# The sums of w_out's quarters: from GpSimd and VectorE to VectorE alone, every second pass, and later in the scheduler's order

## The chip, the cores and the metric

The kernel runs on one core of a Trainium2 chip. The metric is the device time of one execution in microseconds. Times below are the median of several runs where so called; everything that comes from the profile belongs to one profiled execution, which has its own time. Engine names are those of the profile: PE (matrix), DVE (VectorE), ACT (ScalarE), POOL (GpSimd), SP (the engine that issues the DMAs here).

## The reference, cut to what matters

Attention over 8 batches of 8 heads with 512 local tokens and 32 global ones (a local token sees a window of 32 to each side and the global tokens; a global one sees all), then a feed-forward layer over the 4608 tokens:

```python
    attn_out = _attn_ref(**attn_kwargs)                 # 8 x 8 x 544 x 64
    x = np.ascontiguousarray(attn_out.transpose(0, 2, 1, 3)).reshape(B * S, H * D)
    h = x @ w_in                                        # 512 -> 2048
    g = np.where(h > 0.0, h, alpha * (np.exp(np.minimum(h, 0.0)) - 1.0))
    return (g @ w_out).astype(np.float32)               # 2048 -> 512
```

The weights come as 64-bit floats. The kernel splits every value of `x`, of `g` and of the two weights into a high and a low float16 part, scaled by powers of two, and makes each product out of three float16 products.

## The kernel before, in words

**Attention** is a generator of slots (batch, pair of head pairs, tile of 128 tokens). Scores go to PSUM (L626, L574), DVE adds the mask and takes the maximum (L638), ACT makes the exponentials (L645), POOL divides by the sum (L652), PE transposes (L663), the transposed tile is copied to SBUF (L666), and PE multiplies with v (L685). The result is one 256-token block of `x` after the other.

**The feed-forward layer** is a second generator, `ffn_stream`. It works on jobs of one block, and a job on passes: pass `p` (0 to 7) takes the hidden columns of `p` (256 of them). `ffn1` issues 24 matmuls of 128x256 into `h` (L293), then ACT makes `g`, `hs` and the exponential (L302 to L304), DVE joins them (`elu`, L311), ACT makes the high part `gh`, DVE the low part `gl` (L314). Up to `LAG2` = 2 passes later `ffn2` multiplies with w_out, 12 matmuls of 128x512 into two banks `acc` (L368). At the end of a job DVE adds `acc` to the earlier partial result `o` (L376).

**Groups of weights.** w_in and w_out arrive and are converted in four groups of passes: a (0), b (1), c (2, 3), d (4 to 7). Early blocks run one group at a time, and their partial results go to DRAM and back. Once all weights are there, a later block runs all passes in one job, "f", and its second product goes by seven products of 128x256 quarters in place of eight (`ffn2_seven`, L408).

**The sums of quarters** are what these seven products need. `add_up(p, False)`, here called a pair, makes two sums for pass `p` ("rows" and "diag"); `add_up(p, True)`, a cross sum, replaces the middle of w_out's own rows by two differences, and may do so only when no job of the old kind will use pass `p` any more. One call has four steps, each deferred by two ticks against the one before:

- `s0` (L250): `w` = high part + low part of w_out, 128x1024, float16 to float32, on POOL
- `s1` (L254 for a cross sum; L256 and L257 for a pair): the sums or the difference out of `w`, on DVE, 128x512 and 128x256
- `s2` (L261): the high float16 part, on ACT
- `s3` (L265): the low float16 part, on DVE

The tile `w` is one of three buffers named `cu`, of which two hold the diag sums for good, so that only one `w` can be alive. The tiles of `s1` are three buffers named `tmp`. The results lie in `raw` (rows), `cu` (diag) and w_out itself (`wouth`, `woutl`).

**Who calls.** `load()` stands at the head of every pass. Once the table "f" exists it starts one pair if any is left, and one cross sum if its pair was started and pass `p` is free. There are 8 pairs and 8 cross sums.

**What sets the order.** The program is written as the two generators step (by the table `PACE`); small steps are put off by `defer`, and `tick` runs those that are due. The tile layer then orders the instructions of each engine by priority, which is by default the place in the program, and by what it reckons to be ready. `tc.high_priority(offset=n)` moves the instructions inside it n places ahead; a negative n moves them back. On the chip each engine runs its list strictly in order.

Of the kernel before, what the change touches and what calls it, by code (L numbers as in the profile page):

```python
# [29 lines left out]
NP = NFT // 2  # L30
# [7 lines left out]
CONV = 14  # L38
NBL = B * SL // BLK
GROUPS = {"a": (0, 1), "b": (1, 2), "c": (2, 4), "d": (4, 8), "f": (0, 8)}  # L40
NX = 4


# [10 lines left out]
def attn_ffn(ctx: ExitStack, tc: tile.TileContext, qT, qgT, kT, vT, w_in, w_out, mask, out):  # L54
    nc = tc.nc
# [22 lines left out]
    def defer(n, fn):  # L78
        if n == 0:
            return fn()  # L80
        later.setdefault(now[0] + n, []).append(fn)
# [38 lines left out]
    wout = [wz[:, 256:].rearrange("p (f e) -> p f e", f=NFT), wts.tile([P, NFT, DM], F16, name="woutl")]  # L120
# [9 lines left out]
    def load_weights(group):  # L130
        lo, hi = GROUPS[group]
        for p in range(lo, hi):
            for m in range(2):
                unit(m, p)
                if (m, p) == (1, hi - 1):
                    defer(12, lambda: tables(group))
                    if hi == NP:
                        defer(13, lambda: tables("f"))
                yield
# [62 lines left out]
    def tables(group):  # L202

        r = slice(*GROUPS[group])
        wm = wts.tile([P, 4], F32, name=f"wm_{group}")
# [28 lines left out]
    def add_up(p, cross):  # L234


        if not sums:
            sums["rows"] = [ffn.tile([P, NP * 512], F16, name="raw") for _ in range(2)]
            sums["diag"] = [ffn.tile([P, NP * 256], F16, name="cu", bufs=3) for _ in range(2)]
        w = ffn.tile([P, 2, DM], F32, name="cu", bufs=3)  # L240
        s = ffn.tile([P, 512], F32, name="tmp", bufs=3)
        d = None if cross else ffn.tile([P, 512], F32, name="tmp", bufs=3)[:, 0:256]
        pr = slice(2 * p, 2 * p + 2)
        flat = [a[:, pr, :].rearrange("p a b -> p (a b)")[:, 256:768] for a in wout]
        rows = [a[:, p * 512:(p + 1) * 512] for a in sums["rows"]]
        diag = [a[:, p * 256:(p + 1) * 256] for a in sums["diag"]]
        todo = ((flat, s),) if cross else ((rows, s), (diag, d))

        def s0():
            nc.gpsimd.tensor_add(w, wout[0][:, pr, :], wout[1][:, pr, :])  # L250

        def s1():
            if cross:
                nc.vector.tensor_sub(s, w[:, 1, :], w[:, 0, :])  # L254
            else:
                nc.vector.tensor_add(s.rearrange("p (a b) -> p a b", a=2), w[:, :, 0:256], w[:, :, 256:512])  # L256
                nc.vector.tensor_add(d, w[:, 0, 0:256], w[:, 1, 256:512])  # L257

        def s2():
            for dst, src in todo:  # L260
                nc.scalar.copy(dst[0], src)  # L261

        def s3():
            for dst, src in todo:
                nc.vector.tensor_sub(dst[1], src, dst[0])  # L265
            if cross:
                added.append(p)

        for i, fn in enumerate((s0, s1, s2, s3)):
            defer(1 + 2 * i, fn)  # L270

    added = []
    uses = [0] * NP
# [3 lines left out]
    def ffn_stream():  # L277
        pend = []
        state = {}
# [67 lines left out]
        def ffn2():  # L347
            job, p, gh, gl = pend.pop(0)
            group, blk, _, _, sc, seven = job
            first, last = GROUPS[group][0], GROUPS[group][1] - 1  # L350
            if seven is not None:
# [32 lines left out]
        def ffn2_seven(blk, p, gh, gl, sc, done):  # L384
            while p not in added:
                load()
                yield True
# [50 lines left out]
        def split_x(blk):  # L438
            xr, mx = ready[blk]
            xh = ffn.tile([P, NC, BLK], F16, name="xh", bufs=NX)  # L440
            xl = ffn.tile([P, NC, BLK], F16, name="xl", bufs=NX)
            done = []
            xf, hf, lf = (a.rearrange("p c t -> p (c t)") for a in (xr, xh, xl))

            def s1():
                all_max(mx[:, 1:2], mx[:, 0:1])

            def s2():
                nc.vector.tensor_scalar_max(mx[:, 1:2], mx[:, 1:2], LOW)
                power(mx[:, 2:3], mx[:, 1:2])  # L450
                nc.vector.reciprocal(mx[:, 3:4], mx[:, 2:3])
                nc.vector.tensor_scalar_mul(mx[:, 4:5], mx[:, 3:4], 2.0 ** 14)
                nc.scalar.activation(hf, xf, AF.Copy, scale=mx[:, 4:5])  # L453

            def s3():
                nc.vector.scalar_tensor_tensor(out=lf, in0=xf, scalar=mx[:, 4:5], in1=hf,
                                               op0=ALU.mult, op1=ALU.subtract)
                done.append(1)

            nc.vector.tensor_reduce(out=mx[:, 0:1], in_=mx[:, 6:10], op=ALU.max, axis=AX.X)  # L460
            lag = 6 if "f" in tab else 2
            for i, fn in enumerate((s1, s2, s3)):
                defer(lag + i, fn)
            return xh, xl, mx, done

        def scales(group, mx):
            sc = ffn.tile([P, 3 * NP + 1], F32, name="xs", bufs=4)
            wm, t = tab[group]
            o = GROUPS[group]
            r = slice(*o)  # L470
# [11 lines left out]
        def load():  # L482
            if "f" in tab:
                n = state.setdefault("sums", 0)
                if n < NP:
                    add_up(n, False)
                    state["sums"] += 1
                n = state.setdefault("cross", 0)
                first = min((GROUPS["abcd"[step[b]]][0] for b in order if 0 < step[b] < 4), default=NP)
                if n < state["sums"] and not uses[n] and n < first:  # L490
                    add_up(n, True)
                    state["cross"] += 1
            for blk in order:
                if blk in ready and blk not in xs and not step[blk] and len(xs) < NX:
                    xs[blk] = split_x(blk)

        def choose():

            for blk in order:
                if blk in xs and xs[blk][3] and step[blk] < 4:  # L500
                    group = "f" if "f" in tab and not step[blk] else "abcd"[step[blk]]
                    if group in tab:
# [3 lines left out]
                        if seven is None:  # L506
                            for p in range(*GROUPS[group]):
                                uses[p] += 1
# [4 lines left out]
        while lead[0]:  # L513
            load()
            yield True
        while left <= NBL:
            load()
            job = job or choose()
            if job is None:
                yield True  # L520
                continue
            cur, job = job, None
            group, blk = cur[:2]
            lo, hi = GROUPS[group]
            for p in range(lo, hi):
                load()
                yield from ffn1(cur, p)
                if len(pend) > LAG2:
                    yield from ffn2()
                if p == hi - 1:  # L530
                    job = choose()
            if group in "df":
                del xs[blk]
                left += 1
# [6 lines left out]
    def new_x():  # L541
        return ffn.tile([P, NC, BLK], F32, name="xr", bufs=3), ffn.tile([P, 10], F32, name="xm", bufs=NX + 4)

# [315 lines left out]
```

## Time and profile before

| what | value |
|---|---|
| median of 3 runs | 1045.69 us |
| lowest and highest | 1040.73 and 1049.07 us |
| the profiled execution's own time | 1048.61 us |
| its span, first to last instruction | 1046.8 us |
| mean granted PE clock | 0.963 |
| busy: PE, DVE, ACT, POOL | 977.8, 788.2, 687.1, 273.5 us |
| start of the first and the last L250 on POOL | 200.7 and 299.0 us |

The profile is read by stage. The sums lie between about 200 and 375 us of a program of 1047 us, so the shares over the whole span say little of them; what counts is which engine the others wait for in those stretches. "PEclk" is the share of full speed that PE's clock was granted. In the lists of instructions a row is start, duration, engine, line, operation, tiles, and in brackets the idle time ahead of it and what ended that. In the chain of waits a row is start, length and what ran. A duration there is the time until the next link starts, so it is the price of one instruction in a row of many.

### The profile page before, as it was taken

The numbers are of one execution on the slowest core, as the hardware profiler recorded it, in microseconds if no ns is written. First come the engines' busy times: TensorE is split into PE (matmuls) and PEld (weight loads), VectorE is DVE, ScalarE is ACT, GpSimd is POOL, SyncE is SP. The second block draws the span as 40 slices with busy tenths as digits, with TensorE's granted clock in tenths as the row PEclk, the third lists the DMA queues.
The fourth block names the chain that finished last, engine by engine and source line by source line (L and its number), as shares of the span: only waits on it lengthen the run. The fifth ranks groups of instructions, "written<-read, shape, count | busy, mean of one in ns | idle before, by whom it ended". The sixth has DMA issues, their size and how long they took to land.

```text
span 1046.8 us, 21647 instructions
## 1 busy us (share of the span) xinstructions
PE 977.8 (93%) x8128; PEld 781.1 (75%) x8128; DVE 788.2 (75%) x2217; ACT 687.1 (66%) x1561; POOL 273.5 (26%) x458
## 2 busy tenths in 40 slices
PE   6898869889689999999999999999999999999995
PEld 4576546556357678888888888888888888888884
DVE  5789899977865677878786778868787778676573
ACT  4779778655444666667676767667576766677663
POOL 2356574237451112121122112112122121100000
PEclk9799989979689999999999999999999999999998
DMA  7546665531122112311131022101220100000000
GB/s 264 166 127 206 222 224 184 183 112 56 40 76 66 47 41 77 102 27 41 67 102 31 16 90 83 47 22 37 84 89 22 42 21 32 1 22 22 1 22 21
DMA packets 39168, 81.95 MB, mean 78 GB/s; under 512 B 3864, under 2 KB 5912, under 8 KB 39064
## 3 DMA queue, kind: packets, MB, share of 16 engines
q1 hardware_dynamic: 39064, 80.58, 23.5%
q8 instruction: 64, 1.05, 0.4%
q14 instruction: 40, 0.33, 0.1%
HBM read 65.36 MB, written 15.20 MB: 77 GB/s over the span
## 4 chain that ended last, share of the span: by engine, by line
PE 59%; DVE 21%; ACT 11%; issue 3%; POOL 3%; DMA 1%; DVEq 0%; ACTq 0%; POOLq 0%
PE h L293 20%; PE acc L408 9%; PE h L408 5%; PE pa L663 4%; PE pa L626 4%; PE pa L685 4%; ACT p L645 3%; PE pa L293 3%; PE acc L368 3%; DVE p L638 3%; DVE gl L314 3%; DVE g L311 3%; PE pa L574 2%; PE pa L408 2%; ACT g L302 2%
## 5 line engine op out<-in xcount | busy, mean ns | idle before, releaser
L293 PE MATMUL h<-xh,winh 128*128 128x256 f16 x992 | 273.4, 276 | 10.5 <-ACT xh L453 5.9
L293 PE MATMUL h<-xl,winh 128*128 128x256 f16 x992 | 273.2, 275 | 0.1
L293 PE MATMUL h<-xh,winl 128*128 128x256 f16 x992 | 273.0, 275 | 0.0
L293 PEld LDWEIGHTS <-winh 128*128 128x128 f16 x2176 | 213.0, 99 | 51.9 <-issue 22.5
L652 POOL TENSOR_SCALAR p<-p,sm 128x224 f32<-128x224 f32 x256 | 141.8, 573 | 302.9 <-DVE sm L650 145.1
L311 DVE SCALAR_TENSOR_TENSOR g<-g,hs 128x512 f32<-128x512 f32 x136 | 99.8, 734 | 98.5 <-ACT g L304 97.7
L645 ACT ACTIVATE p<-p,m 128x224 f32<-128x224 f32 x256 | 120.2, 472 | 70.7 <-DVE m L641 69.3
L408 PEld LDWEIGHTS <-gh 128*128 128x128 f16 x1456 | 141.8, 98 | 21.0 <-issue 4.8
L302 ACT ACTIVATE g<-h,xs 128x512 f32<-128x512 f32 x124 | 85.0, 685 | 55.7 <-PE h L293 55.1
L293 PEld LDWEIGHTS <-winl 128*128 128x128 f16 x1088 | 107.4, 99 | 13.7 <-issue 0.4
L314 DVE SCALAR_TENSOR_TENSOR gl<-gs,xs,gh 128x640 f16<-128x640 f32 x104 | 94.2, 906 | 23.1 <-ACT gh L333 22.9
L333 ACT ACTIVATE gh<-gs,xs 128x640 f16<-128x640 f32 x104 | 86.4, 831 | 38.3 <-DVE gs L329 38.3
L332 ACT ACTIVATE gh<-g,xs 128x256 f16<-128x256 f32 x104 | 53.3, 513 | 77.2 <-DVE g L311 77.2
L304 ACT ACTIVATE g<-g 128x512 f32<-128x512 f32 x136 | 85.9, 632 | 0.0
L303 ACT ACTIVATE hs<-h,xs 128x512 f32<-128x512 f32 x124 | 84.8, 684 | 0.0
L663 PE MATMUL pa<-ident,p 128*128 128x128 f32 x512 | 79.6, 283 | 4.1 <-POOL p L652 4.0
L314 DVE SCALAR_TENSOR_TENSOR gl<-g,xs,gh 128x256 f16<-128x256 f32 (+1 forms) x136 | 77.7, 572 | 4.6 <-ACT gh L318 4.4
L408 PEld LDWEIGHTS <-gl 128*128 128x128 f16 x728 | 71.2, 98 | 13.0 <-DVE gl L314 0.5
L638 DVE CUSTOM_DVE_ANT_0 p<-pa,msk 128x224 f32<-128x224 f32 x228 | 76.5, 383 | 4.6 <-PE pa L626 4.5
L408 PE MATMUL acc<-raw,gh 128*128 128x256 f16 x416 | 79.4, 273 | 0.0
L666 DVE COPY pt<-pa 128x512 f32<-128x512 f32 x98 | 66.6, 680 | 13.8 <-PE pa L663 13.7
L626 PE MATMUL pa<-k,q 64*128 64x224 f32 x456 | 68.5, 400 | 3.2 <-ACT pt L666 2.2
(194 smaller groups left out, 2048.5 us busy)
## 6 DMA issues: line engine op xcount, KB each, us to landing
v<-vT SPq DMA_DIRECT2D x64, 256.0 KB, 2.7
k<-kT SPq DMA_DIRECT2D x32, 448.0 KB, 4.0
out<-o SPq DMA_DIRECT2D x34, 256.0 KB, 2.1
q<-qT SPq DMA_DIRECT2D x32, 256.0 KB, 5.0
raw<-w_in SPq DMA_DIRECT2D x8, 1024.0 KB, 6.0
raw<-w_out SPq DMA_DIRECT2D x8, 1024.0 KB, 5.3
od<-o SPq DMA_DIRECT2D x24, 256.0 KB, 2.5
o<-od SPq DMA_DIRECT2D x24, 256.0 KB, 3.3
```

Source lines behind the costliest of these rows:

```text
L293: nc.tensor.matmul(h[:, j, :], wt[:, c, f], xt[:, c, :], start=k == 0, stop=k == 11)
L302: nc.scalar.activation(g, hf, AF.Relu, scale=sc[:, p:p + 1])
L304: nc.scalar.activation(g, g, AF.Exp, scale=-1.0)
L311: nc.vector.scalar_tensor_tensor(out=g, in0=g, scalar=-1.0, in1=hs, op0=ALU.add, op1=ALU.max)
L314: nc.vector.scalar_tensor_tensor(out=dst, in0=src, scalar=sg, in1=hi, op0=ALU.mult, op1=ALU.subtract)
L333: nc.scalar.activation(gh[:, 2:7, :], s, AF.Copy, scale=sg)
L408: nc.tensor.matmul(cols, gt, w, start=first, stop=p == NP - 1 and k == len(todo) - 1)
L626: nc.tensor.matmul(sp[r][:, j * KW:(j + 1) * KW], q[rows, t * P:(t + 1) * P], k[rows, t, :], start=True, stop=True)
L638: nc.vector.tensor_tensor_reduce(out=p[:, 0:KW], in0=sp[r][:, j * KW:(j + 1) * KW], in1=msk[:, mi, :], op0=ALU.add, op1=ALU.max, scale=1.0 ...
L645: nc.scalar.activation(ps[i][:, 0:KW], ps[i][:, 0:KW], AF.Exp, bias=m[:, 1, i:i + 1], scale=scale, accum_out=s[:, 0, i:i + 1])
L652: nc.gpsimd.tensor_scalar(ps[i][:, 0:KW], ps[i][:, 0:KW], s[:, 1, i:i + 1], 1.0, ALU.mult, ALU.mult)
L663: nc.tensor.transpose(tp[:, (2 * r + i) * P:(2 * r + i + 1) * P], ps[2 * j + r][:, i * P:(i + 1) * P], ident)
```

## The change

Three things are changed: `s0` is issued on DVE in place of POOL; all four steps of a sum are issued under a priority of 60 places further back; and `load()` starts a pair at every second call only (a cross sum still at every call, once its conditions hold).

```diff
@@ -38,6 +38,7 @@
+BEHIND = 60
@@ -247,7 +248,7 @@
         def s0():
-            nc.gpsimd.tensor_add(w, wout[0][:, pr, :], wout[1][:, pr, :])
+            nc.vector.tensor_add(w, wout[0][:, pr, :], wout[1][:, pr, :])
@@ -266,8 +267,12 @@
+        def behind(fn):
+            with tc.high_priority(offset=-BEHIND):
+                fn()
+
         for i, fn in enumerate((s0, s1, s2, s3)):
-            defer(1 + 2 * i, fn)
+            defer(1 + 2 * i, lambda fn=fn: behind(fn))
@@ -482,7 +487,8 @@
         def load():
             if "f" in tab:
                 n = state.setdefault("sums", 0)
-                if n < NP:
+                state["turn"] = not state.get("turn")
+                if n < NP and state["turn"]:
                     add_up(n, False)
                     state["sums"] += 1
```

Line numbers after the change are higher by one to six: L250, L254, L265, L311, L314 and L376 become L251, L255, L266, L316, L319 and L381. DVE's list has 16 instructions more, POOL's 16 fewer, and PE's list is in the same order from about 240 us on. From the pass whose tile is `g_3744` on DVE's list is the same but for names.

The first of two places is DVE, one pass in the middle of the sums. The names carry buffer numbers: a `tmp` made from a `cu` is `s1`, a `raw`, `cu` or `woutl` made from a `tmp` is `s3`. Before:

```order
L311 SCALAR_TENSOR_TENSOR g_2876<-g_2876,hs_2877 128x512
L265 TENSOR_TENSOR raw_2771<-tmp_2842,raw_2770 128x512
L265 TENSOR_TENSOR cu_2773<-tmp_2843,cu_2772 128x256
L314 SCALAR_TENSOR_TENSOR gl_2882<-g_2876,xs_2700,gh_2881 128x512
L265 TENSOR_TENSOR woutl_109<-tmp_2845,wouth_107 128x512
L256 TENSOR_TENSOR tmp_2911<-cu_2910 128x512
L257 TENSOR_TENSOR tmp_2912<-cu_2910 128x256
L254 TENSOR_TENSOR tmp_2914<-cu_2913 128x512
L311 SCALAR_TENSOR_TENSOR g_2945<-g_2945,hs_2946 128x512
```

And now, the same pass:

```order
L316 SCALAR_TENSOR_TENSOR g_2866<-g_2866,hs_2867 128x512
L257 TENSOR_TENSOR tmp_2895<-cu_2894 128x512
L258 TENSOR_TENSOR tmp_2896<-cu_2894 128x256
L319 SCALAR_TENSOR_TENSOR gl_2872<-g_2866,xs_2700,gh_2871 128x512
L251 TENSOR_TENSOR cu_2897<-wouth_107,woutl_109 128x1024
L266 TENSOR_TENSOR raw_2771<-tmp_2895,raw_2770 128x512
L255 TENSOR_TENSOR tmp_2898<-cu_2897 128x512
L266 TENSOR_TENSOR cu_2773<-tmp_2896,cu_2772 128x256
L251 TENSOR_TENSOR cu_2962<-wouth_107,woutl_109 128x1024
L316 SCALAR_TENSOR_TENSOR g_2929<-g_2929,hs_2930 128x512
```

Both `w` of a pass (`cu_2897`, `cu_2962`) now stand in DVE's list, each between the steps that need it and those that free its buffer. `gl` is two rows behind `g` where it was three.

The second place is DVE again, some five passes on, at a block's low part `xl` (beside it stand steps of attention). Before, no step of a sum stands within this stretch; `s1` of three late cross sums stood a few rows ahead of it. Now:

```order
L257 TENSOR_TENSOR tmp_3626<-cu_3625 128x512
L647 TENSOR_SCALAR m_3320<-m_3320 128x4
L107 TENSOR_SCALAR xm_2504<-xm_2504 128x1
L258 TENSOR_TENSOR tmp_3627<-cu_3625 128x256
L456 RECIPROCAL xm_2504<-xm_2504 128x1
L251 TENSOR_TENSOR cu_3864<-wouth_107,woutl_109 128x1024
L457 TENSOR_SCALAR xm_2504<-xm_2504 128x1
L266 TENSOR_TENSOR raw_2771<-tmp_3626,raw_2770 128x512
L255 TENSOR_TENSOR tmp_3865<-cu_3864 128x512
L251 TENSOR_TENSOR cu_3970<-wouth_107,woutl_109 128x1024
L461 SCALAR_TENSOR_TENSOR xl_3251<-xr_2503,xm_2504,xh_3250 128x1024
```

The last pair (`cu_3625`) and two of the late cross sums have moved to the front of `xl`, which is on the way of the next block into the feed-forward layer. Over the nine passes from `g_2809` to `g_3484` DVE's list holds 13 times L251, `s1` of 7 pairs and 6 cross sums, and `s3` of 8 pairs and 4 cross sums.

## The prediction

> **What bounds the kernel now.** I read the page's slices first, to find the stretch in which PE isn't full, then the table by windows for that stretch, and then the instructions in it.
>
> ```profile
> span 1046.8 us, 21647 instructions
> PE   6898869889689999999999999999999999999995
> DVE  5789899977865677878786778868787778676573
> ```
>
> A slice is 26.2 us. From the thirteenth on (314 us) PE is at nine tenths or more in all but the last slice; up to there it is not. The sums of w_out lie in slices 8 to 12, and the eleventh (262 to 288 us) has PE at 6 beside DVE at 8.
>
> ```profile
> core 0: us, PE busy (x) PEld busy (x) DVE busy (x) ACT busy (x) POOL busy (x), PEclk, DMA share, GB/s
> 251.00:260.00 9.00, 9.00 (x66) 6.35 (x65) 6.70 (x10) 4.26 (x8) 4.97 (x3) 1.00 0.01 2
> 260.00:269.00 9.00, 5.70 (x18) 2.06 (x17) 8.65 (x10) 3.84 (x8) 4.55 (x3) 0.69 0.00 0
> 269.00:278.00 9.00, 3.10 (x23) 2.39 (x22) 9.00 (x12) 4.40 (x9) 5.08 (x3) 0.88 0.00 1
> ...
> 241.00:322.00 81.00, 65.48 (x411) 41.54 (x410) 61.23 (x106) 37.56 (x80) 40.09 (x33) 0.85 0.21 66
> 322.00:343.00 21.00, 21.00 (x159) 14.68 (x160) 10.48 (x26) 10.78 (x25) 2.87 (x7) 1.00 0.09 26
> ```
>
> From 260 to 278 us DVE is busy 17.65 of 18 us and PE gets through 41 matmuls, at a reduced clock. Between 322 and 343 us PE is full at full clock: 21.00 us for 159 matmuls, 0.132 us each. At that price the 411 matmuls from 241 to 322 us are 54.3 us of work, in a stretch of 81: **about 26 us are lost to PE there**. The chain of waits gives the same price from another side:
>
> ```profile
> 235.89 2.62 PE h L293 x24
> ...
> 348.31 2.59 PE acc L368 x12
> ```
>
> A pass of the feed-forward layer is 24 + 12 matmuls, 5.21 us. Nine of them are 46.9 us; what attention puts between them makes up the rest of 54.3. Who makes PE wait is told by the groups of this stretch:
>
> ```profile
> L368 PE MATMUL acc<-wouth,gl 128*128 128x512 f16 x35 | 15.8, 451 | 2.8 <-DVE gl L314 2.8
> L368 PE MATMUL acc<-wouth,gh 128*128 128x512 f16 x34 | 15.1, 443 | 9.0 <-DVE o L376 8.5 <-ACT gh L318 0.5
> ```
>
> It is DVE each time, with steps that cost it 0.7 us and come late. Late behind what, the list of DVE and POOL shows:
>
> ```profile
> 259.51 2.50 POOL L250 TENSOR_TENSOR cu<-wouth,woutl 128x1024 f32<-128x1024 f16 x1 [0.81 <-DVE tmp L254]
> 277.52 2.12 POOL L250 TENSOR_TENSOR cu<-wouth,woutl 128x1024 f32<-128x1024 f16 x1 [2.56 <-DVE tmp L257]
> ...
> 259.35 0.69 DVE L311 SCALAR_TENSOR_TENSOR g<-g,hs 128x512 f32<-128x512 f32 x1
> 259.95 2.61 DVE L265 TENSOR_TENSOR raw<-tmp,raw 128x512 f16<-128x512 f32 x1
> 275.43 0.68 DVE L265 TENSOR_TENSOR raw<-tmp,raw 128x512 f16<-128x512 f32 x1
> 277.96 2.22 DVE L311 SCALAR_TENSOR_TENSOR g<-g,hs 128x512 f32<-128x512 f32 x1
> ```
>
> The same instruction takes 0.68 us alone and 2.61 us when it starts inside an L250 of POOL; L311 takes 0.69 and 2.22. Each of the two long ones ends within 0.6 us of the end of POOL's. So while POOL adds, a DVE instruction with two operands in SBUF stands still. Where none of these falls into an L250, DVE waits for its result (the waits of this stretch, with us in total, times, longest; the two rows below it are used further down):
>
> ```profile
> DVE tmp L254 <- POOL cu L250: 9.3, 4, 2.7
> PE acc L368 <- DVE o L376: 8.5, 3, 6.0
> ...
> DVE raw L265 <- ACT raw L261: 0.4, 1, 0.4
> ```
>
> Either way **an addition on POOL costs DVE about 2 us**, two of them a pass, and a pass takes 9 us (L311 starts at 259.35 and, two passes later, at 277.96) where PE needs 5.2.
>
> The Trainium skill, "SBUF — State Buffer", on the two sides of SBUF, says that DVE and GpSimd share a pair of ports as an exclusive lock, held for a whole instruction, and that a DVE instruction with two SBUF inputs falls under it; the trace agrees, 2.22 against 0.69 us.
>
> **The change part by part.** *Taken from POOL.*
>
> ```profile
> L250 POOL TENSOR_TENSOR cu<-wouth,woutl x16: 2117/2124/2507, 200.7 to 299.0; 128x1024 f32<-128x1024 f16 x16
> ```
>
> Fourteen of the 16 start after 241 us. At 2 us each DVE gets back 28 us of standing still, close to the 26 us that PE loses. POOL has nothing else that is waited for in the FFN-only passes.
>
> *Added to DVE.* A 128x1024 addition of two float16 tiles into float32 isn't in the trace on DVE. The nearest rows, as prices in a row of work:
>
> ```profile
> 203.40 0.60 DVE cu L163
> 205.32 1.14 DVE cu L166
> 211.82 0.60 DVE tmp L256
> 277.04 0.34 DVE tmp L257
> 263.50 0.66 DVE gl L314
> 268.51 0.60 DVE g L311
> ```
>
> L166 has two tensors of 128x1024, 1.14 us; L163 has one, 0.60 us. From 256 to 512 columns (L257, L256) the price grows by 0.26 us, which carried on to 1024 gives 0.60 + 0.53 = 1.13. I take 1.14, since two tensors are read; 0.60 is the lower end.
>
> The Trainium skill, "VectorE: DVE Perf Modes", on what auto-detection checks, lets an instruction with two tensors run at double rate only if every tensor is 16-bit; the float32 result here would rule that out. By it the price stays at 1.14; with the double rate, 13 additions would give DVE 7 us back.
>
> *Moved on DVE.* I price its list over the nine passes from `g_2809` to `g_3484`, which before are the stretch from 241 to 322 us. Sums: 13 L251 at 1.14 = 14.8; `s1` of 7 pairs at 0.94 = 6.6 and of 6 cross sums at 0.60 = 3.6; `s3` of 8 pairs at 0.94 = 7.5 and of 4 cross sums at 0.60 = 2.4. Together 34.9 us. The rest of DVE's work there is as before:
>
> ```profile
> L314 DVE SCALAR_TENSOR_TENSOR gl<-g,xs,gh 128x512 f16<-128x512 f32 x10 | 8.9, 893 | 0.0
> L311 DVE SCALAR_TENSOR_TENSOR g<-g,hs 128x512 f32<-128x512 f32 x9 | 7.9, 877 | 0.0
> L376 DVE SCALAR_TENSOR_TENSOR o<-acc,xs,o 128x512 f32<-128x512 f32 x5 | 3.6, 739 | 0.0
> L666 DVE COPY pt<-pa 128x512 f32<-128x512 f32 x4 | 2.7, 681 | 1.8 <-PE pa L663 1.8
> L638 DVE CUSTOM_DVE_ANT_0 p<-pa,msk 128x224 f32<-128x224 f32 x8 | 2.7, 385 | 0.6 <-PE pa L626 0.6
> ```
>
> At undisturbed prices `gl` is 6.6 and `g` 5.4; with the three others 21.0 us, and I put the small ones (a block's `xl`, reductions, statistics) at 4. Sum: 34.9 + 25 = **60 us of DVE against 54 us of PE**. So DVE stays the bound of this stretch, by little, and PE should be short of work by some 6 us in place of 26. In a pass without attention such as `g_2866` to `g_2929`, DVE has 6.1 us against PE's 5.2; over the first five passes 27 against 26, which the two passes of lead of `ffn1` can hide; the passes before and at `xl_3251` have 7 to 9 us of DVE, beside attention's matmuls on PE.
>
> *The waits.* Both engines near full, each hand-off can cost. The added wait is none by itself: `w` is now freed and refilled within one engine, where POOL and DVE took turns. What is left is `s3`, which waits for ACT's cast. Before, that cost 0.4 us in all; behind it now stand `gl`, `o` and the next `w`, and PE waits for the first two. I put 3 us for such waits, half a hand-off a pass, between 0 and 12. So the stretch takes 60 + 3 = 63 us in place of 81: **-18**.
>
> *Before 241 us.* Two additions fall into the conversion of the last weights, and DVE is on the chain there with both instructions that they hold up:
>
> ```profile
> 201.22 2.18 DVE g L311
> 213.58 2.00 DVE gl L314
> ```
> ```profile
> 238.62 0.73 DVE L311 SCALAR_TENSOR_TENSOR g<-g,hs 128x512 f32<-128x512 f32 x1 [1.59 <-ACT g L304]
> ```
>
> Undisturbed these are 0.60 and 0.66, so 2.9 us come back; two additions of 1.14 go in, the first on the chain in place of 0.94 that moves behind it, the second ahead of the 1.59 us for which DVE idles before 238.62. **-2**, between 0 and -4.
>
> *Every second pass.* The pairs now spread over eight passes and not seven: the scheduler takes them ahead again where it sees DVE free. Priced in the list above, so nothing more. *The place 60 back*: `gl` two rows behind `g`, not three; in the list too.
>
> *After 322 us* PE is full (21.00 of 21.00), and its list is the same, so the time saved stays saved; late cross sums leave DVE 10.5 of 21 us busy there, and it can take the lag up.
>
> Sum, against the profiled execution's 1048.6 us: -18 - 2 = 1028.6, which is 1.9% less. The median shown lies 2.9 us below that execution; carried over, the prediction is **1026 us**.
>
> **The rivals.** *PE becomes the bound at once.* If the addition costs 0.60 us, DVE's 60 us fall to 53, and the stretch is PE's 54.3: -26 with -3 before it, 1017. For it speaks that PE is full right after; against it the two-tensor row of 1.14.
>
> *DVE keeps PE waiting.* DVE has more work than PE, and a stall of 2.8 us at 261 us was followed by a granted clock of 0.69. If `o` and `gl` still come late at each of the five `o`, waits are 12 us and not 3: -9 and 0, 1037. For it: `o` alone made PE wait 8.5 us. Against it: 6.0 of these were one wait in which POOL held DVE several times.
>
> *Slower: `s3` holds DVE.* DVE's list is strict. If each cast stands in ACT's list behind the three ACT instructions of a pass, DVE waits for these first:
>
> ```profile
> 383.20 0.69 ACT g L302
> 383.89 0.58 ACT hs L303
> 384.46 0.53 ACT g L304
> ```
>
> That is 1.8 us for each of the 20 `s3` (8 pairs of two, 4 cross): 36 us, 60 + 36 = 96 in place of 81, and with -2 that makes 1059. It decides from (81 - 60) / 20 = 1.05 us a cast. Against it: in the list, `gl`, another `s1` or a `w` stand between most `s1` and their `s3`, and ACT was busy only 37.56 of 81 us.
>
> *The gain is given back.* Were something later bound by transfers or by the pace of attention, the 20 us would turn into idle time there: 1046. Against it speaks the full PE after 322 us.
>
> **How the numbers follow.** A measurement of this kernel can tell about 1% from no change, which is 1035.2 us. Chances: the forecast (1020 to 1033) 0.60; PE the bound 0.13; PE kept waiting 0.17, about half of it under 1035; given back 0.06; slower 0.04. So faster by over 1% 0.81, within 1% 0.15, slower 0.04. The range is 1016 to 1038: from the faster addition to five late `o`; beyond it lie the last two cases.
>
> **What would show it.** POOL without L250 and no `g` or `gl` over 1 us in the whole trace; L251 on DVE at 1.1 to 1.2 us; from 241 us to `g_3484` 60 to 66 us, with DVE over 90% busy; the eleventh slice of PE at 8 or 9 and its clock near 10; the same PE rate after. Wrong would be: `s3` long idle for ACT, PE waiting over 10 us for `o` and `gl` together, or the saved time coming up as idle PE after 330 us.

## The result, and the profile after

| | before | after |
|---|---|---|
| median | 1045.28 us (4 runs) | 1017.18 us (4 runs, 1015.35 to 1018.12) |
| ratio, with its 95% interval | | 0.9731 (0.9689 to 0.9772) |
| the profiled execution's own time | 1048.61 us | 1018.12 us |
| busy: PE, DVE, ACT, POOL | 977.8, 788.2, 687.1, 273.5 us | 965.1, 785.8, 685.9, 247.0 us |
| mean granted PE clock | 0.963 | 0.977 |

The kernel is 28 us faster, where 20 were forecast: the time lies within the range (1016 to 1038), at its fast end, and outside the 1020 to 1033 that had been called the likeliest. The page of the kernel after, span and slices:

```profile
span 1016.3 us, 21648 instructions
...
PE   6898879989999999999999999999999999999994
...
DVE  5789898999986778677777778787787878766663
...
PEclk9799999989999999999999999999999999999998
```

The hole in PE's row (the 6 and the 8 from 262 us on) is gone, and DVE is at 9 in the slices of the sums up to the eleventh. The windows of the nine passes, which now run from 234.9 to 294.6 us, and of the stretch behind them:

```profile
core 0: us, PE busy (x) PEld busy (x) DVE busy (x) ACT busy (x) POOL busy (x), PEclk, DMA share, GB/s
...
235.00:295.00 60.00, 58.45 (x423) 39.84 (x422) 59.83 (x121) 37.96 (x83) 15.86 (x19) 1.00 0.26 85
295.00:312.00 17.00, 17.00 (x132) 11.93 (x130) 10.19 (x27) 9.49 (x22) 4.49 (x7) 1.00 0.09 28
```

DVE has 59.83 of 60 us busy, and still PE is full but for 1.55 us, at full clock. The same instructions on DVE as shown before, and what PE and DVE waited for:

```profile
L251 DVE TENSOR_TENSOR cu<-wouth,woutl x16: 1191/1212/1239, 209.8 to 295.7; 128x1024 f32<-128x1024 f16 x16
```

```profile
257.18 0.68 DVE L316 SCALAR_TENSOR_TENSOR g<-g,hs 128x512 f32<-128x512 f32 x1
...
259.70 0.68 DVE L266 TENSOR_TENSOR raw<-tmp,raw 128x512 f16<-128x512 f32 x1
```

```profile
PE pa L112 <- DVE xm L465: 1.0, 1, 1.0
DVE gl L319 <- ACT gh L323: 1.0, 1, 1.0
...
PE acc L373 <- DVE o L381: 0.4, 1, 0.4
```

The addition takes 1.21 us on DVE where it took 2.12 on POOL; in the nine passes no `g`, `gl` or step of a sum is longer than the shortest of its kind by more than 0.26 us; `s3` (L266) waits for ACT not once, and PE waits for DVE 1.4 us in place of 15. The 15 are the 8.5 and 2.8 us of the prediction's groups and the first of these two waits of the kernel before; the second one, like the 9.3 us shown there, is a wait of DVE for POOL's addition:

```profile
PE pa L111 <- DVE xm L460: 3.7, 1, 3.7
...
DVE tmp L256 <- POOL cu L250: 2.3, 1, 2.3
```

One sign that the prediction named did not come true: in the whole trace three `g` and `gl` still take over 1 us (1.25, 1.12 and 1.52, at 162.5, 169.6 and 184.4 us). Beside each of them stands a clamp of the weights on POOL (L160, one input, 1.04 to 1.10 us).

**Where the 28 us came from**, read from the starts of four L311 (L316 after): the one three passes ahead of `g_2742`, `g_2742` itself, `g_2809`, and the one at the end of the nine passes.

| kernel | three passes ahead | `g_2742` | `g_2809` | end of nine | the nine passes |
|---|---|---|---|---|---|
| before | 196.0 | 238.6 | 241.3 | 322.4 | 81.1 |
| before, second profile | 195.1 | 236.6 | 239.4 | 319.6 | 80.3 |
| before, third profile | 193.6 | 234.7 | 237.4 | 317.6 | 80.2 |
| after | 195.5 | 231.7 | 234.9 | 294.6 | 59.6 |

Against the second and third profile the stretch up to `g_2742` went from 41.3 to 36.2 us (5 us), the nine passes from 80.2 to 59.6 (21), and the three passes behind them from 20.3 to 17.8 (2.5; the L311 after them starts at 339.9 in the second profile and at 312.3 after).

### The profile page after: what moved, and what is told of

Read it like the earlier page. It is cut to its first block, busy times and chain, and to the rows that moved or that the text cites. A ratio compares the mean times of both kernels' runs of the same rounds, so it can differ in the third digit from the quotient of the medians.

```text
span 1016.3 us, 21648 instructions
## 1 busy us (share of the span) xinstructions
PE 965.1 (95%) x8128; PEld 775.3 (76%) x8128; DVE 785.8 (77%) x2233; ACT 685.9 (67%) x1561; POOL 247.0 (24%) x442
## 4 chain that ended last, share of the span: by engine, by line
PE 60%; DVE 21%; ACT 13%; issue 3%; POOL 1%; DMA 1%; DVEq 0%; ACTq 0%; POOLq 0%
PE h L298 20%; PE acc L413 9%; PE h L413 5%; PE pa L691 4%; PE pa L669 4%; PE pa L632 4%; ACT p L651 4%; PE pa L298 3%; DVE p L644 3%; PE pa L580 2%; DVE gl L319 2%; PE acc L373 2%; DVE g L316 2%; PE pa L413 2%; ACT g L307 2%
## 5 line engine op out<-in xcount | busy, mean ns | idle before, releaser
L298 PEld LDWEIGHTS <-winh 128*128 128x128 f16 x2176 | 211.6, 99 | 49.4 <-issue 20.3
L658 POOL TENSOR_SCALAR p<-p,sm 128x224 f32<-128x224 f32 x256 | 144.1, 580 | 333.5 <-DVE sm L656 191.3
L316 DVE SCALAR_TENSOR_TENSOR g<-g,hs 128x512 f32<-128x512 f32 x136 | 96.2, 707 | 96.2 <-ACT g L309 95.5
L319 DVE SCALAR_TENSOR_TENSOR gl<-gs,xs,gh 128x640 f16<-128x640 f32 x104 | 94.2, 905 | 23.1 <-ACT gh L338 22.9
L319 DVE SCALAR_TENSOR_TENSOR gl<-g,xs,gh 128x256 f16<-128x256 f32 (+1 forms) x136 | 75.0, 552 | 5.3 <-ACT gh L323 5.1
L669 PEld LDWEIGHTS pa<-ident,p 128*128 128x128 f32 x512 | 61.5, 145 | 10.5 <-POOL p L658 6.2
```

The lines of the kernel that those rows point to most:

```text
L298: nc.tensor.matmul(h[:, j, :], wt[:, c, f], xt[:, c, :], start=k == 0, stop=k == 11)
L316: nc.vector.scalar_tensor_tensor(out=g, in0=g, scalar=-1.0, in1=hs, op0=ALU.add, op1=ALU.max)
L319: nc.vector.scalar_tensor_tensor(out=dst, in0=src, scalar=sg, in1=hi, op0=ALU.mult, op1=ALU.subtract)
L658: nc.gpsimd.tensor_scalar(ps[i][:, 0:KW], ps[i][:, 0:KW], s[:, 1, i:i + 1], 1.0, ALU.mult, ALU.mult)
L669: nc.tensor.transpose(tp[:, (2 * r + i) * P:(2 * r + i + 1) * P], ps[2 * j + r][:, i * P:(i + 1) * P], ident)
```

## The experiments

Each starts from one of the two kernels and changes one thing, or nothing. The main theory: an instruction of POOL that reads SBUF stops DVE's instructions with two SBUF operands, so that the move to DVE carries the gain. Its rivals: the sums were too dense (then the spreading carries it), or POOL and DVE lost time by taking turns at the one buffer `w`.

**The move alone.**

```diff
-            nc.gpsimd.tensor_add(w, wout[0][:, pr, :], wout[1][:, pr, :])
+            nc.vector.tensor_add(w, wout[0][:, pr, :], wout[1][:, pr, :])
```

> Only s0 moves to DVE; pairs at every pass and the usual priority. If an addition on POOL stops DVE for its length, this one line brings most of the gain: DVE's list over the nine passes of the sums is priced at 58 us as in the changed kernel, but 33 us of it fall into the first five passes, where PE has 26, so DVE lags by 7 us there and PE waits a little: 1019 to 1026 us. If what mattered is that the sums are spread out (every second pass, lower priority), most of the gain is missing: 1035 us or more.

Measured: 1019.98 us, ratio 0.9776 (0.9743 to 0.9809), nine passes 58.7 us. The one line brings some 25 of the 28 us. In its profile PE waits 3.9 us for `o`, where it waited 0.4 in the changed kernel:

```profile
L368 PE MATMUL acc<-wouth,gh 128*128 128x512 f16 x44 | 16.7, 379 | 3.9 <-DVE o L376 3.9
```

**The spreading alone**, with the sums left on POOL:

```diff
-            nc.vector.tensor_add(w, wout[0][:, pr, :], wout[1][:, pr, :])
+            nc.gpsimd.tensor_add(w, wout[0][:, pr, :], wout[1][:, pr, :])
```

> The changed kernel with s0 back on POOL: only every second pass and the place 60 back. If POOL's additions stop DVE, 13 of them at 2 us replace 14.8 us of DVE work in the nine passes: 60 - 15 + 26 = 71 us in place of 81 before and 60 after, and the stretched instructions before the stretch stay: 1032 to 1040 us. If spreading made the gain: 1017 to 1022 us.

Measured: 1045.05 us, ratio 1.0016 (0.9995 to 1.0037), nine passes 79.9 us. Spreading gains nothing by itself, not even the 4 to 12 us that I expected. Its windows, waits and POOL's additions (the last two rows say who waited for them, with us and times):

```profile
260.00:280.00 20.00, 10.79 (x45) 5.31 (x46) 16.41 (x24) 8.18 (x16) 8.48 (x4) 0.70 0.11 41
280.00:300.00 20.00, 13.71 (x102) 9.26 (x99) 14.69 (x29) 9.25 (x23) 12.92 (x7) 0.93 0.08 26
```

```profile
POOL cu L251 <- DVE tmp L258: 18.6, 7, 4.5
...
DVE tmp L255 <- POOL cu L251: 10.9, 5, 2.3
```

```profile
L251 POOL TENSOR_TENSOR cu<-wouth,woutl x16: 2114/2127/2774, 200.5 to 297.3; 128x1024 f32<-128x1024 f16 x16
...
  DVE tmp L255: 10.9, 5
  DVE tmp L257: 4.2, 2
```

Fourteen of the 16 additions still sit in the stretch. DVE waits 15.1 us for their results, and seven of its instructions are together 11.9 us longer than others of their kind: 27 us, 1.9 for each addition, close to the 2 that I had put. The kernel before shows the same two costs in its nine passes, 11.6 us of such waits (9.3 and 2.3) and 16.5 us in eleven longer instructions, 2.0 us for each of 14. What my 71 us left out are some 8 us for which DVE waits there for PE and ACT, as it does in the kernel before: 45 us of other work, 27 and 8 make 80, and 79.9 were measured.

**Without the lower priority, and without every second pass.**

```diff
-            defer(1 + 2 * i, lambda fn=fn: behind(fn))
+            defer(1 + 2 * i, fn)
```

> The changed kernel without the place 60 back. Its lists differ from the changed kernel's by seven rows on DVE and a few on ACT, none of them gl or g: both theories expect the same time as the changed kernel, 1015 to 1020 us. More than 1022 us would mean that the order of these few rows carries the gain.

```diff
-                if n < NP and state["turn"]:
+                if n < NP:
```

> The changed kernel with a pair at every pass. DVE's list in the first five passes is 30 us against PE's 26 and in the changed kernel's 27, total the same: a lag of 4 us, which the lead of two passes can hide: 1016 to 1021 us if DVE's sum decides, 1030 us or more if spreading does.

Measured: 1018.05 us, ratio 0.9753 (0.9711 to 0.9794), and 1019.72 us, ratio 0.9769 (0.9731 to 0.9806). The nine passes take 59.7 and 58.3 us. The two kernels with a pair at every second pass (this first one and the changed kernel) stand at 1018.1 and 1017.2 us, the two with a pair at every pass (the second one and the move alone) at 1019.7 and 1020.0. So every second pass may be worth some 2 us, which is at the edge of what these runs tell apart, and the place 60 back nothing that shows.

**Idle additions on POOL.** The changed kernel, and two instructions on POOL beside each sum, whose result nobody reads (the line that makes the tile `spare` is left out here; `s` is the `tmp` of the sum):

```diff
+            for _ in range(2):
+                nc.gpsimd.tensor_add(spare, s, s)
```

> The changed kernel, and beside each sum two additions on POOL that nobody needs (128x512 of a tmp with itself, about 1.06 us each by half of L250's 2.12), so 32 in all, 26 of them in the nine passes where DVE has no idle time. If a two-input instruction on POOL stops DVE's two-input instructions for its length, DVE loses up to 26 us there and the time goes back to 1035 to 1047 us, though no result of POOL is waited for. If the cost before was that POOL and DVE took turns at the one buffer w, nothing is lost: 1016 to 1021 us.

Measured: 1036.64 us, ratio 0.9911 (0.9877 to 0.9944), nine passes 76.6 us. DVE's list is the same and it waits for none of POOL's results. Its instructions and POOL's:

```profile
251.99 1.52 DVE L319 SCALAR_TENSOR_TENSOR g<-g,hs 128x512 f32<-128x512 f32 x1
253.44 0.68 DVE L269 TENSOR_TENSOR woutl<-tmp,wouth 128x512 f16<-128x512 f32 x1
...
257.93 1.21 DVE L252 TENSOR_TENSOR cu<-wouth,woutl 128x1024 f32<-128x1024 f16 x1
...
260.60 2.06 DVE L252 TENSOR_TENSOR cu<-wouth,woutl 128x1024 f32<-128x1024 f16 x1
```

```profile
L261 POOL TENSOR_TENSOR spare<-tmp x32: 1034/1368/2008, 233.1 to 342.9; 128x512 f16<-128x512 f32 x32
```

A held instruction is up to 0.84 us longer than usual (1.52 against 0.68, 2.06 against 1.21): POOL's 1.03 us less 0.2. In the nine passes, beside 26 idle additions, 25 instructions are longer than others of their kind, 19 of them by 0.73 to 0.85 us, and all together by 17.5 us; the nine passes grew by 17.0. All 25 have two operands in SBUF. An `o` (L384), which reads one of its two operands from PSUM, kept its 0.74 us at 267.55, beside POOL's addition that ends at 268.52. Turn-taking has no part in it, so that rival falls for this cost. It does not fall for the 11.6 us that DVE waited for results in the kernel before: those are turns at `w`, which the move to DVE ended as well, and no run gave the sums a second `w` to part the two costs.

**Idle instructions with one input.**

```diff
+            for _ in range(2):
+                nc.gpsimd.tensor_scalar(spare, s, 1.0, 1.0, ALU.mult, ALU.mult)
```

> The same with instructions of one input on POOL (a tensor_scalar of 128x512, about 1 us by L652's 0.45 for 224 columns). By the rule of the Trainium skill, SBUF - State Buffer, any GpSimd instruction that reads SBUF holds the shared ports, so it would cost as much as the additions: 1035 us or more. By the trace of before, where an L265 beside four L652 took 0.68 us as always, it costs nothing: 1016 to 1021 us.

Measured: 1026.22 us, ratio 0.982 (0.9792 to 0.9848), nine passes 67.9 us: 9 us over the changed kernel, between the two answers. Here are DVE's instructions and POOL's:

```profile
248.37 1.09 DVE L319 SCALAR_TENSOR_TENSOR g<-g,hs 128x512 f32<-128x512 f32 x1
...
249.38 0.68 DVE L269 TENSOR_TENSOR woutl<-tmp,wouth 128x512 f16<-128x512 f32 x1
...
255.69 1.62 DVE L252 TENSOR_TENSOR cu<-wouth,woutl 128x1024 f32<-128x1024 f16 x1
```

```profile
L261 POOL TENSOR_SCALAR spare<-tmp x32: 618/930/4865, 232.4 to 332.7; 128x512 f16<-128x512 f32 x32
```

Here the hold is 0.41 us, POOL's 0.62 less 0.2 again. Twenty longer instructions make 7.4 of the 8.3 us by which the nine passes grew; once DVE also waits, 1.2 us, for a `tmp` that an idle instruction still reads. So one input is enough. The Trainium skill, "SBUF — State Buffer", in the section on the two sides of SBUF, asks of the GpSimd instruction only that it reads SBUF, and the trace agrees. The price is lower than I had put because the instruction takes 0.62 us and not 1. My counter-evidence, an L265 of 0.68 us beside four L652, was read wrongly: in these four it seems to be POOL that waited.

```profile
229.47 1.74 POOL L652 TENSOR_SCALAR p<-p,sm 128x224 f32<-128x224 f32 x4 [11.85 <-DVE wm_f L208]
...
234.36 2.25 POOL L652 TENSOR_SCALAR p<-p,sm 128x224 f32<-128x224 f32 x4
```

That is the kernel before: four L652 took 1.74 us beside short DVE work and 2.25 beside the L265.

**The first two additions.** The kernel before with two of 16 on DVE:

```diff
-            nc.gpsimd.tensor_add(w, wout[0][:, pr, :], wout[1][:, pr, :])
+            (nc.vector if p == 0 else nc.gpsimd).tensor_add(w, wout[0][:, pr, :], wout[1][:, pr, :])
```

> The kernel before with only the first pair's and the first cross sum's s0 on DVE, the two that start at 200.7 and 212.9 us; the other 14 stay on POOL. In the changed kernel the pass of g_2742 came 6.9 us earlier, of which I had worked out 2. If the two held-up instructions on the chain are the cause of all 6.9, this kernel has g_2742 at 231 to 233 us and 1037 to 1040 us in all. If the rest came from another order of PE's list there, g_2742 is at 235 to 237 us and the time 1041 to 1044.

Measured: 1042.16 us, ratio 0.9977 (0.996 to 0.9993), `g_2742` at 233.4 us, 36.2 us after the marker. The place was close to the first answer, the time as in the second. Since one profile of before was little to go by, I took the kernel before twice more, and this one once more:

> The kernel before, unchanged, for a second profile. It tells how much of the 6.9 us that the changed kernel is ahead at g_2742 belongs to the one profiled execution of before: from the L311 at 196.0 to that of g_2742 it took 42.6 us, with the sums' first two additions on POOL. If the two held-up instructions cost what they seem, the stretch takes 41 to 43 us again; if that execution was an odd one, it takes 37 to 39.

> The kernel before once more, a third profile, with the same two answers: 41 to 43 us, or 37 to 39.

> The kernel before with the first two additions on DVE, a second profile. The first had 36.2 us for that stretch, as the changed kernel, and yet the runs were only 0.1 to 0.4% faster than before. If the gain of the stretch is real, 36 to 37 us again, and 320 us or less at the end of the nine passes (before: 322.4); if it is scatter, 39 us or more.

Measured from the marker to `g_2742`: 41.5 and 41.1 us for before (42.6 in its first profile), 36.2 again with two additions on DVE; and the times of these three single executions were 1045.96, 1043.80 and 1040.42 us. The end of the nine passes came at 314.2 us in the last, where 320 or less was expected of a real gain. So 5 us of that stretch belong to the two additions, and about 1 us to the first profile of before. The other kernels agree: 36.1 us in the move alone, 41.1 with the spreading alone. What they do there is shown by a window and PE's wait, first of before (second profile):

```profile
213.00:230.00 17.00, 16.41 (x84) 11.20 (x84) 12.45 (x47) 8.59 (x24) 5.05 (x9) 0.62 0.30 83
```

```profile
209.72 0.45 PE L111 MATMUL pa<-ident,cm 128*128 128x128 f32 x1 [3.49 <-DVE m L641]
```

Then of the kernel with two additions on DVE (second profile):

```profile
213.00:230.00 17.00, 17.00 (x126) 11.97 (x126) 14.92 (x61) 13.61 (x41) 7.65 (x13) 0.96 0.45 148
```

```profile
207.05 0.29 PE L111 MATMUL pa<-ident,cm 128*128 128x128 f32 x1 [1.99 <-DVE m L641]
```

Beside the held L311 PE waits 3.49 us in place of 1.99, and in the window behind it PE has a granted clock of 0.62 in place of 0.96 and 84 matmuls in place of 126. The other profiles of before have 0.60 and 0.70 with 66 and 91 matmuls there, the first of this kernel 0.86 with 109. The second held instruction falls into the same window, so what the wait alone did isn't shown. In the whole time 0.7 to 4.2 us of the 5 are seen (the interval of the ratio); the nine passes, with 14 additions still on POOL, stay at 80.8 us. From the marker to its end the program takes 846.4 and 846.5 us in the two profiles of this kernel and 850.2 to 852.6 in the three of before, so some 4 us stay; where the marker itself lies scatters between 193.6 and 197.2 us.

**A shorter lead.** The changed kernel with one pass of lead between the two products while the sums are made:

```diff
-                if len(pend) > LAG2:
+                while len(pend) > (1 if "f" in tab and group != "f" else LAG2):
                     yield from ffn2()
```

> The changed kernel with ffn1 leading ffn2 by one pass in place of two while the sums are made (jobs of group f keep two). I had PE short by 6 us of work and 3 us of waits in the nine passes, and it lost 1.5. If the lead of two passes is what hid DVE's lag, PE idles here by 5 to 15 us between 235 and 312 us, and the time is 1022 to 1032 us. If DVE had no lag to hide, the time stays at 1016 to 1020.

Measured: 1017.65 us, ratio 0.9736 (0.9705 to 0.9766), nine passes 59.8 us.

```profile
235.00:312.00 77.00, 75.96 (x560) 52.19 (x559) 69.97 (x152) 45.33 (x99) 17.10 (x26) 1.00 0.22 71
```

PE idles for 1.04 us of 77. My theory that the lead of two passes hides DVE's lag falls: there is no lag that one pass would not hide as well.

**Another instruction of POOL.** The changed kernel with the clamp of the weights on DVE too:

```diff
-            nc.gpsimd.tensor_scalar(u, u, FMAX, FMIN, ALU.min, ALU.max)
+            nc.vector.tensor_scalar(u, u, FMAX, FMIN, ALU.min, ALU.max)
```

> The changed kernel with the other large instruction of POOL moved too: the clamp of a weight's magnitudes (L160, 128x1024 float32, one input, 16 times, 1.04 us) on DVE, where a tensor_scalar of this size takes 0.60 us. By the runs with idle instructions on POOL, a one-input instruction of 1.04 us stops DVE for 0.4 to 0.8 us if a two-input instruction is due, so the change is worth between -3 and +3 us on DVE and nothing on PE where DVE isn't late: 1014 to 1020 us. Faster than 1013 us would mean that DVE bounds the conversion of the weights through POOL's holds.

Measured: 1021.51 us (1015.12 to 1023.6), ratio 0.978 (0.9748 to 0.9812): no gain over the changed kernel, and just outside the 1014 to 1020 us expected. Its marker is 7 us late (202.9 us) and the nine passes take 58.6 us, and `g_2809` is 4 us late, so what it loses it loses while the weights are converted. Why stays open. No run was found that beats the changed kernel.

## Why the prediction was right, and where its sizes were off

- **The bound and the mechanism were right.** DVE bound the stretch, because POOL's additions stopped it or made it wait, at 2.0 us each as put (16.5 us of longer instructions and 11.6 of waits for 14 additions; they are 1.6 a pass, where the prediction says two). The move alone gives 25 of 28 us, the spreading alone none, and idle work on POOL brings 19 us back.
- **The price of the addition was right**: 1.14 us was taken, and L251 is 1.21 us long, with the next instruction 1.13 to 1.14 us after its start. The rival that named 1017 us named it for an addition of 0.60 us, which is not what happened; its condition, PE full at once, came true by another way.
- **The sum over the nine passes was right for DVE, wrong for PE.** Sixty us of DVE were forecast, 59.6 measured. What failed is "PE should be short of work by some 6 us": it was short by 1.55. The 54.3 us of PE work came from the mean price of a matmul in a stretch with another mix (0.132 us); the matmuls of these passes come to 0.138, and there are more of them (58.45 us for 423 in the window, where before had 411). Both engines had the same load, and neither waited much for the other. The forecast time did not rest on this step: it went by DVE's 60 us.
- **The waits**, put at 3 us, were nothing: `s3` never waited for ACT. The rival "slower", by the wait for ACT's casts, is thereby out; so is the rival in which DVE keeps PE waiting. Without this term the stretch is 21 us shorter, not 18. Nor did DVE wait for PE and ACT as it had before, some 8 us: the sum had put nothing for that, and DVE's list kept it busy for 59.83 of 60 us.
- **Before 241 us** the term was -2 and came out at -5. I had priced the two held instructions and not what comes with a late DVE there: PE's wait of 3.49 us and the low clock behind it (0.60 to 0.70 in three profiles of before and in the spreading alone, 0.86 to 1.00 in every kernel with these two on DVE). How the other 3 us are shared out isn't shown.
- **After 322 us** nothing was expected, and 2.5 us were gained: the three passes behind the sums took 17.8 us in place of 20.3. The term counted what is kept and not that PE is further ahead of DVE at this point. Counted from the program's start to the L311 at the end of the nine passes, PE has done 1777 matmuls in each of the three profiles of before and 1795 after; three passes on it is 1931 in all four. PE is full there in both kernels and has 18 fewer left to do, which at 0.13 us each is 2.3 of the 2.5 us. So this gain was made earlier and only shows here; some eight of the 18 had been done by `g_2809`.
- That the saved time would be given back later was ruled out: the 30.3 us between the two profiles at the end of those three passes are 30.5 at the end of the program.

By terms: -5, -21 and -2.5, with 0.5 us lost between `g_2742` and `g_2809`, make -28, against a measured -28.1. The fastest rival's 1017 us equals the measured time by chance: its cause, an addition of 0.60 us, did not occur, and 3 us of waits that were not there, 3 more before the stretch and 2.5 behind it make up the difference to 1026.

## What to carry to other kernels

An elementwise instruction isn't free on GpSimd just because GpSimd is idle: look whether VectorE's instructions beside it are longer than the same ones elsewhere, and whether they end with GpSimd's. If they do, the GpSimd instruction costs VectorE about its own length, and moving it there can pay even when VectorE is the busier engine: here 1.14 us replaced about 2. When two engines are near the same load, price both with their own rows of that very stretch: the larger sum is the forecast, and the smaller one says whether the other engine will wait.

## What was not expected of the hardware

- The hold is nearly the whole of GpSimd's instruction, in all three forms seen: up to 0.84 us by a 1.03 us instruction with two inputs, 0.41 us by a 0.62 us one with one, and 1.93 us (2.61 against 0.68) by an L250 of the kernel before, which undisturbed takes 2.12. With the idle additions, two of which often stand in a row, no held instruction was longer by more than 0.85 us.
- It goes both ways. In the run with idle additions, four L661 (the division, 1.74 us undisturbed in the kernel before) took 5.66 us:

```profile
288.89 5.66 POOL L661 TENSOR_SCALAR p<-p,sm 128x224 f32<-128x224 f32 x4
```

- With two instructions of DVE held between 200 and 216 us, PE's granted clock from 213 to 230 us was 0.62 and not 0.96, with 42 matmuls fewer in this window. Whether PE's wait, longer by 1.5 us, is what lowered it is not shown.
